# Round-by-round order in the first layer's batched stage, and reordered copies at the border of the linear layers

## The chip, the cores and the metric

The kernel runs on one core of one Trainium2 chip. The metric is the device time of one execution in microseconds (us). Seven executions of the kernel before lie between 3771.52 and 3776.72 us; their median is 3774.59 us. One execution was also taken with the hardware profiler, and every duration in this document that is not called a median comes from such a profiled execution.

## What is computed

Four layers act in turn on x of 2048 rows by 640: attention with a recurrent memory (A), linear attention (B), A again, B again. Each adds its result to x and takes the layer norm of x as input. Cut to what matters here:

```
def _A_ref(x, mem0, Wq, Wk, Wv, Wo, seg_len):      # 64 segments of 32 rows, 8 memory rows, 32 heads of 192
    mem = mem0
    for s in range(n_seg):
        h = concatenate([mem, xs])                  # 40 rows by 640
        q, k, v = h @ Wq, h @ Wk, h @ Wv            # 640 to 6144 each
        p = softmax(where(mask, q k^T * scale, -1e9))
        o = (p v) @ Wo
        mem = o[:8]; outs.append(o[8:])

def _B_ref(x, wqkv, w_phi, wo):                     # 32 heads of 20
    q, k, v = x @ wqkv
    phi_q, phi_k = softmax features of q and k, both signs
    o = (phi_q (phi_k^T v)) / (phi_q sum(phi_k))
    return o @ wo
x = x + A(layernorm(x)); x = x + B(layernorm(x))    # twice
```

The memory rows make the segments of an A layer a chain: segment s+1 needs the output of segment s.

## The kernel before

**The A layer has two stages.** A segment has 8 memory rows and 32 rows of x. The memory rows and the first 24 rows are projected in the chain; the last 8, the "tail" rows, do not depend on the memory and are projected ahead for many segments at once. `A_pre` does that: it takes the tail rows of 32 segments (256 rows, called a half, h = 0 or 1) through Wk, Wq and Wv. The weights are cut into four rounds r of 8 heads. One half with one round is called a half-round here: 12 groups of matmuls for K and Q (line 787, 10 matmuls of 128x256 a group), 8 groups for V (line 804, 5 matmuls of 128x384 a group), so 20 PSUM banks to empty. There are 8 PSUM banks in the pool. `evict` empties a bank by a copy, VectorE (line 87) and ScalarE (line 89) in turn. After K and Q of a half-round ScalarE's queue issues one write of `kqb` to memory (line 793, 1536 KB); after each V pair GpSimd's queue issues four writes of `vb` (line 808). `A_chain` then runs the 64 segments one after another; it is most of the kernel.

**The order of `A_pre` is written by hand** (`manual_schedule`). Before the change the loop over halves is outside and the loop over rounds inside: half 0 takes rounds 0, 1, 2, 3, half 1 takes 3, 2, 1, 0. `load_matrix` issues the weights of a round on SP's queue as the code reaches it. Most pieces have a home of their own; three of the five pieces of each matrix for rounds 0 and 3 share a slot, so that what round 3 put into the slots is replaced by round 0 at the very end (9 loads again).

**Layer norm as tasks.** In the first layer the norms are made inside this stage. `tails(1)` loads the tail rows of half 1 (line 691, four loads on ScalarE's queue and four on GpSimd's), `all_rows` norms all 16 blocks of 128 rows. One block is four tasks: load, moments (line 221 on VectorE, 225 and 227 on GpSimd), deviation (lines 234 and 235 on ScalarE), apply and store (lines 241 to 244, store on GpSimd, line 747). After every evict one task is taken from the list: 2 blocks of tails and 16 of rows are 72 tasks. Blocks use two buffers in turn. In the kernel before, the list is filled when half 0 comes to its third round. At the start of a half its rows are transposed by two groups of five matmuls (line 166), whose banks go out through the same copies; every group of that half needs them.

**A semaphore for a DMA.** DMAs that SP and ScalarE issue share eight semaphores, given out in one sequence for both queues; the instruction that issues a DMA waits until the last DMA with that semaphore has landed. This is in the built program's wait lists, as software sets them.

**The border to a B layer.** `post_steps` finishes the tail rows of the A layer at the head of `layer_B`. For each of four blocks tb of 16 segments, `fetch` loads `otb` (line 1117, SP) into `ot` and copies it into the layout `ow` (four copies on VectorE and ScalarE, lines 87 and 89); `multiply` runs 96 matmuls (lines 1129 and 1130), copies the result out (lines 1132 and 1133) and stores it (line 1135, SP). Blocks use two buffers in turn. Beside this, `norm_rows` (line 359 loads attention rows on SP, line 360 adds on GpSimd, then the norm; the last scaling is line 246 on ScalarE) prepares the rows of group 0, and `turn_rows` transposes them: 5 matmuls of line 166 into one of three banks, emptied on ScalarE (line 89). Here a scheduler decides the order on the engines, from data dependence and its own estimate of time, so rows of group 1 can be put before those of group 0 wherever it thinks them ready. Groups are 512 rows; the body of the layer is `for g in range(NG)`.

Of the kernel before, what the change touches and what calls it, by code (L numbers as in the profile page):

```python
# [8 lines left out]
P = 128  # L9
BF16 = mybir.dt.bfloat16  # L10
F32 = mybir.dt.float32
# [104 lines left out]
class Kernel:  # L116
# [131 lines left out]
    def layer_B(self, x_dram, at_dram, xout_dram, xnext_dram, li, bp, post):  # L248
# [44 lines left out]
        with tc.tile_pool(name=f"B{li}_kv", bufs=1, space=bass.MemoryType.PSUM, reuse_waits="tile") as kvp, \  # L293
# [71 lines left out]
            def turn_rows(b, xn, xnT):  # L365
                pt = bank("ps_x", BF16)
                for k in range(KC):
                    self.transp(out=pt[:, P * k:P * k + P], in_=xn[:, P * k:P * k + P], identity=self.ident[:, :])
                q = P * (b % 4)
                self.ev.copy(out=xnT[:, :, q:q + P], in_=pt[:, 0:D].rearrange("p (k t) -> p k t", t=P), eng="s")  # L370

            def new_xnT():
                return xnTs.next().rearrange("p (k t) -> p k t", k=KC)
# [1 line left out]
            def norm_T(g):  # L375
                xnT = new_xnT()
                load_rows(g)
                for b in range(4 * g, 4 * g + 4):
                    turn_rows(b, norm_rows(b), xnT)
                return xnT  # L380
# [73 lines left out]

            with tc.issue_after(self.last_load.ins):
                load_rows(0)
            fetch, multiply = post
            ow = [fetch(tb) for tb in range(2)]
            for j in (1, 2, 0):
                nc.sync.dma_start(out=wqkv[:, :, D * j:D * j + D],  # L460
                                  in_=self.B_wqkv.rearrange("(k p) n -> p k n", p=P)[:, :, D * j:D * j + D])
            multiply(0, ow[0], kv_ps[0], side_bank("ps_post"))
            ow.append(fetch(2))
            rows = [norm_rows(b) for b in range(4)]
            multiply(1, ow[1], kv_ps[1], side_bank("ps_post"))
            ow.append(fetch(3))
            multiply(2, ow[2], kv_ps[0], side_bank("ps_post"))
            first_xnT = new_xnT()
            for b in range(4):
                turn_rows(b, rows[b], first_xnT)  # L470
            multiply(3, ow[3], kv_ps[1], side_bank("ps_post"))
            waiting = None
            for g in range(NG):
                xnT = first_xnT if g == 0 else norm_T(g)
                if g == 1:
                    late_constants()
                keys_values(g, xnT)
                if waiting is not None:
                    query_features(*waiting)
                waiting = (g, heads_T(xnT, 0, "qT"))  # L480
# [179 lines left out]
    def A_pre(self, xn_dram, li, load_matrix, piece, wo_mid, wo_end, lay_out_wo, early_wo, x_raw):  # L660
# [3 lines left out]
        NR = 4  # L664
# [8 lines left out]
        with ExitStack() as es:  # L673
# [14 lines left out]
            def gather(dst, src, h, k):  # L688
                xv = src.rearrange("(s t) d -> t s d", t=32)
                for t2 in range(TP):  # L690
                    (nc.gpsimd if k % 2 else nc.scalar).dma_start(out=dst[SH * t2:SH * t2 + SH, :], in_=xv[24 + TP * k + t2, SH * h:SH * h + SH])

            def columns(h):
                return xT[h][:, 0:KC * T].rearrange("p (b t) -> p b t", t=T)
# [38 lines left out]
            def evict(out, in_):  # L733
                ev.copy(out=out, in_=in_)
                if tasks:
                    tasks.pop(0)()
# [3 lines left out]
            def tails(h):  # L740
                return in_turn([norm_tasks(lambda x, k=k: gather(x, x_raw, h, k),
                                           lambda xn, k=k: normed.__setitem__((h, k), xn), "ln_xt") for k in range(NT)])
# [13 lines left out]
                    for f in step:  # L756
                        f()
            turn = nv = 0
            for h in range(NH):
                xBT = columns(h)  # L760
                for k in range(NT):
                    if x_raw is not None:
                        xb = normed[h, k]
                    else:
                        xb = xB[h][k % 2]
                        gather(xb, xn_dram, h, k)
                    transpose_rows(xb, h, k)

                if h == NH - 1:
                    lay_out_wo()  # L770
                for ri, r in enumerate(range(NR) if h == 0 and NH > 1 else range(NR - 1, -1, -1)):
                    st = sts[turn % 2]
                    turn += 1
                    if x_raw is not None and h == 0 and ri == 1:
                        self.build_A_consts()
                    if x_raw is not None and h + 1 < NH and ri == 2:
                        tasks += tails(h + 1)
                        tasks += all_rows()
                    for mi, m in enumerate("KQ"):
                        load_matrix(m, r)  # L780
                        w = [piece(m, r, b) for b in range(KC)]
                        for c0 in range(0, 12, CB):
                            ps = ps_.tile([P, 512], F32, name="ps_pre", tag="bank")
                            for i in range(CB):
                                c = c0 + i
                                for b in range(KC):
                                    nc.tensor.matmul(ps[:, T * i:T * i + T], lhsT=w[b][:, P * c:P * c + P], rhs=xBT[:, b, :],
                                                     start=(b == 0), stop=(b == KC - 1))
                            G, xi = c0 // 6, c0 % 6
                            so = st[:, :, 96 * mi:96 * mi + 96].rearrange("p s (i g t) -> p i g s t", g=2, t=8)  # L790
                            evict(out=so[:, xi:xi + CB, G],
                                  in_=ps[:, :].rearrange("p (i t s) -> p i s t", i=CB, t=8))
                    nc.scalar.dma_start(out=self.kqb_d[SH * h:SH * h + SH, :, r, :].rearrange("s p f -> p s f"), in_=st)
                    load_matrix("V", r)
                    if h == NH - 1 and ri == NR - 1:
                        early_wo()
                    w = [piece("V", r, b) for b in range(KC)]
                    for k in range(NT):
                        vt = vts[nv % 2]
                        nv += 1  # L800
                        for g in range(4):
                            ps = ps_.tile([P, 512], F32, name="ps_pre", tag="bank")
                            for b in range(KC):
                                nc.tensor.matmul(ps[:, 0:384], lhsT=xBT[:, b, P * k:P * k + P],
                                                 rhs=w[b][:, 384 * g:384 * g + 384], start=(b == 0), stop=(b == KC - 1))
                            evict(out=self.two_heads(vt[:, g, :]), in_=ps[:, 0:384].rearrange("p (e f) -> p e f", e=2))
                        for t2 in range(TP):
                            nc.gpsimd.dma_start(out=self.vb_d[SH * h:SH * h + SH, r, :, TP * k + t2, :],
                                                in_=vt[SH * t2:SH * t2 + SH, :, :].rearrange("p (g x) f -> p g (x f)", x=2))
            assert not tasks  # L810
        if x_raw is None:
            self.small.close()
# [295 lines left out]
    def post_steps(self, ops):  # L1108

        nc = self.nc  # L1110
        at_dram, wo_mid, wo_end, low = self.post_args
        wo = [wo_end[:, :], wo_mid[:, 0:7680], wo_mid[:, 7680:15360], low[:, 0:7680]]

        def fetch(tb):
            o = 7680 + 12288 * (tb % 2)
            ot = low[:, o:o + 6144].rearrange("p (s f) -> p s f", f=384)
            nc.sync.dma_start(out=ot, in_=self.otb_d[16 * tb:16 * tb + 16].rearrange("s p f -> p s f"))
            ow = low[:, o + 6144:o + 12288].rearrange("p (c q) -> p c q", q=P)
            for k in range(4):
                self.ev.copy(out=ow[:, 12 * k:12 * k + 12, :].rearrange("p c (s t) -> p c s t", t=8),  # L1120
                             in_=ot[:, :, 96 * k:96 * k + 96].rearrange("p s (c t) -> p c s t", t=8))
            return ow

        def multiply(tb, ow, p0, p1):
            for c in range(48):
                lhsT = ow[:, c, :]
                w0 = 640 * (6 * (c % 2) + c % 12 // 2)
                w = wo[c // 12][:, w0:w0 + 640]
                nc.tensor.matmul(p0[:, :], lhsT=lhsT, rhs=w[:, 0:512], start=(c == 0), stop=(c == 47))  # L1129
                nc.tensor.matmul(p1[:, 0:128], lhsT=lhsT, rhs=w[:, 512:640], start=(c == 0), stop=(c == 47))  # L1130
            ob = ops.tile([P, 640], BF16, name="obB", tag="obB", bufs=2)
            nc.vector.tensor_copy(out=ob[:, 0:512], in_=p0[:, :])
            nc.scalar.activation(out=ob[:, 512:640], in_=p1[:, 0:128], func=ACT.Copy)
            av = at_dram.rearrange("(s t) d -> s t d", t=32)
            nc.sync.dma_start(out=av[16 * tb:16 * tb + 16, 24:32, :], in_=ob[:, :])

        return fetch, multiply


# [33 lines left out]
```

## Time and profile before

| what | value |
|---|---|
| median of seven runs | 3774.59 us |
| the profiled execution's own time | 3773.25 us |
| span of its profile | 3771.5 us |
| TensorE busy | 3549.9 us (94% of the span) |
| VectorE, ScalarE, GpSimd busy | 2362.1, 2074.8, 1664.9 us |
| mean granted TensorE clock | 0.977 |
| A_pre of the first layer, first to last matmul | 14.65 to 211.2 us |
| four multiplies and the transposes, first border | 1597.9 to 1661.4 us |
| four multiplies and the transposes, second border | 3459.0 to 3523.9 us |

The span runs from the first to the last instruction; 1.75 us of the execution lie around it. In a timeline, a line gives start, duration, engine, source line, operation, output and input, shape and how many were merged, and in square brackets how long the engine had stood idle and what ended that. "ACTq" and "SPq" are issues of DMAs on an engine's queue. Times of one stage can be compared line by line; a share of the whole span hides a stage that takes 5% of it.

### The profile page before, as it was taken

Reading aid. Unit: us, or ns where it says so; the run is one execution under the profiler, and the core shown is the slowest. Engines: PE = TensorE matmul, PEld = TensorE weight load, DVE = VectorE, ACT = ScalarE, POOL = GpSimd, SP = SyncE. Lnnn points to the kernel's source line nnn. Section 1 sums busy time; section 2 is a strip of 40 time slices with the busy share of each in tenths; the row PEclk is TensorE's granted clock in tenths of the full one; section 3 lists DMA queues with packets and bytes.
Section 4 is the critical chain, followed back from the end, with each engine's and each line's share of the span. In section 5 each row is a group of like instructions: output and inputs, shape, how many; then the busy total and the mean of one; then the engine's idle time right before and its main releaser. Section 6 shows DMA issues by size and latency. Waiting matters only on the chain. (4 is left out here: it accounts for less than half of the span.)

```text
span 3771.5 us, 169092 instructions
## 1 busy us (share of the span) xinstructions
PE 3549.9 (94%) x71064; PEld 2321.1 (62%) x71408; DVE 2362.1 (63%) x6290; ACT 2074.8 (55%) x5285; POOL 1664.9 (44%) x4367
## 2 busy tenths in 40 slices
PE   7889999999999999989899899999999999999798
PEld 5666666666666666645367566666666666665453
DVE  3546666666666666545643566666666666664565
ACT  2246666656666666536432566666666666664453
POOL 2435555555555555430342455555555554554300
PEclk9989999999999999989899999999999999999899
DMA  9778787878888787840376878888787887889100
GB/s 327 245 253 294 272 298 274 294 276 281 295 281 295 273 293 277 309 127 1 125 252 197 298 275 286 288 280 293 276 294 273 291 283 276 294 279 313 50 1 29
DMA packets 532613, 935.26 MB, mean 248 GB/s; under 512 B 141178, under 2 KB 298378, under 8 KB 531850
## 3 DMA queue, kind: packets, MB, share of 16 engines
q1 hardware_dynamic: 393898, 805.73, 60.2%
q0 software_dynamic: 68288, 88.95, 7.8%
q10 hardware_dynamic: 69664, 29.76, 3.0%
q8 instruction: 558, 9.14, 1.0%
q14 instruction: 205, 1.68, 0.1%
HBM read 855.97 MB, written 72.09 MB: 246 GB/s over the span
## 5 line engine op out<-in xcount | busy, mean ns | idle before, releaser
L885 PE MATMUL ps_qk<-arena,hT 128*32 128x384 bf16 x20480 | 1001.1, 328 | 22.4 <-DMA arena<-in_A_Wk_dram 7.9
L885 PEld LDWEIGHTS <-hT 128*32 128x32 bf16 x30720 | 738.0, 96 | 440.3 <-DVE hT L1103 28.9
L895 ACT ACTIVATE raw<-ps_qk 128x384 bf16<-128x384 f32 x1024 | 503.0, 491 | 391.7 <-PE ps_s L993 250.3
L961 PE MATMUL ps_w<-arena,OT 128*32 128x160 bf16 x24576 | 541.5, 235 | 23.2 <-issue 14.6
L868 POOL DMA_DIRECT2D Vp<-vb x512 | 258.7, 505 | 656.8 <-PE ps_o L935 452.3
L885 PE MATMUL ps_v<-arena,hT 128*32 128x384 bf16 x10240 | 535.5, 329 | 0.0
L961 PEld LDWEIGHTS <-OT 128*32 128x32 bf16 x24576 | 435.2, 97 | 115.9 <-issue 38.5
L900 DVE STREAM_TRANSPOSE KT<-raw 128x384 bf16<-128x384 bf16 x512 | 296.1, 578 | 202.2 <-ACT raw L895 198.2
L903 DVE STREAM_TRANSPOSE QT<-raw 128x256 bf16<-128x256 bf16 x512 | 227.9, 445 | 239.4 <-ACT raw L895 198.0
L856 POOL DMA_DIRECT2D kqb<-kqb x512 | 290.0, 566 | 165.7 <-POOL KT L864 148.1
L916 DVE CAST Vp<-ps_v 64x384 bf16<-64x384 f32 x512 | 286.2, 559 | 89.5 <-ACT Vp L914 76.3
L954 POOL DMA_DIRECT2D otb<-otb x512 | 282.5, 552 | 115.8 <-DVE otb L950 98.3
L914 ACT ACTIVATE Vp<-ps_v 64x384 bf16<-64x384 f32 x512 | 246.3, 481 | 148.0 <-PE ps_v L885 109.0
L941 DVE CAST OT<-ps_o 128x192 bf16<-128x192 f32 x512 | 183.2, 358 | 215.9 <-PE ps_o L935 198.1
L1000 DVE TENSOR_TENSOR E<-E,ps_s 80x320 bf16<-80x320 bf16 x512 | 247.5, 483 | 73.5 <-ACT ps_s L999 69.5
L979 ACT ACTIVATE E<-ps_s 80x320 bf16<-80x320 f32 x512 | 221.9, 433 | 126.7 <-PE ps_s L927 98.4
L935 PEld LDWEIGHTS <-Vp 80*128 80x128 bf16 x4096 | 183.7, 99 | 160.2 <-issue 121.6
L935 PE MATMUL ps_o<-E,Vp 80*128 80x80 bf16 x4096 | 234.3, 202 | 26.2 <-ACT Vp L914 5.7
L927 PE MATMUL ps_s<-QT,KT 128*80 128x80 bf16 (+1 forms) x3072 | 234.0, 213 | 20.3 <-DVE KT L900 11.6
L849 ACT ACTIVATE Vp<-ps_w 32x160 bf16<-32x160 f32 x512 | 150.7, 294 | 171.2 <-DVE wt L1102 151.6
L940 ACT ACTIVATE OT<-ps_o 128x192 bf16<-128x192 f32 x512 | 167.8, 328 | 140.0 <-PE ps_o L935 140.0
L927 PEld LDWEIGHTS <-KT 128*80 128x80 bf16 x3072 | 195.9, 119 | 69.1 <-issue 60.4
(148 smaller groups left out, 5468.1 us busy)
## 6 DMA issues: line engine op xcount, KB each, us to landing
arena<-wo_rows SPq DMA_DIRECT2D x792, 320.0 KB, 6.8
arena<-in_A_Wq_dram SPq DMA_DIRECT2D x430, 384.0 KB, 4.5
arena<-in_A_Wv_dram SPq DMA_DIRECT2D x430, 384.0 KB, 6.4
arena<-in_A_Wk_dram SPq DMA_DIRECT2D x768, 192.0 KB, 4.7
kqb<-arena ACTq DMA_DIRECT2D x16, 1536.0 KB, 8.7
kqb<-kqb POOLq DMA_DIRECT2D x512, 48.0 KB, 5.1
arena<-in_A_Wk_dram SPq DMA_DIRECT2D x46, 384.0 KB, 7.3
vb<-arena POOLq DMA_DIRECT2D x128, 112.0 KB, 5.5
```

The costliest lines, as they stand in the source:

```text
L856: nc.gpsimd.dma_start(out=kqb[:], in_=self.kqb_d[s, :, r, :])
L868: nc.gpsimd.dma_start(out=Vs[n % 2][64:80, :], in_=self.vb_d[s, r].rearrange("g t f -> (g t) f"))
L885: nc.tensor.matmul(o[32 * g:32 * g + 32, 0:384], lhsT=hT[:, b, :], rhs=rhs, start=(i == 0), stop=(i == KC - 1), tile_position=(0, 32 * g), ...
L895: nc.scalar.activation(out=raw[:], in_=ps[:, 0:384], func=ACT.Copy)
L900: nc.vector.transpose(out=KT[:, :, 0:64], in_=raw[:, :].rearrange("p (c j) -> p c j", j=64))
L914: nc.scalar.activation(out=o, in_=i, func=ACT.Copy)
L916: nc.vector.tensor_copy(out=o, in_=i)
L927: nc.tensor.matmul(S[0:80, c0:c0 + 80 * (q1 - q0)], lhsT=KT[:, 3 * x + i, :], rhs=QT[:, x, q0:q1, :], start=False, stop=(x == 1 and i == 2 ...
L935: nc.tensor.matmul(O[x][:, 80 * i:80 * i + 80], lhsT=Vs[n % 2][0:80, 448 * x + k:448 * x + k + 128], rhs=E[0:80, 160 * x + 80 * e:160 * x ...
L954: nc.gpsimd.dma_start(out=self.otb_d[s, :, 96 * r:96 * r + 96], in_=otb[:, :, :].rearrange("p c t -> p (c t)"))
L961: nc.tensor.matmul(W[32 * g:32 * g + 32, 0:160], lhsT=OT[:, c, q:q + 32], rhs=w[:, 640 * i + 160 * g:640 * i + 160 * g + 160], start=(firs ...
L1000: nc.vector.tensor_tensor(out=E[0:80, 0:320], in0=E[0:80, 0:320], in1=rc, op=ALU.mult)
```

## The change

1. In the first layer, `A_pre` walks `(h, r)` with the rounds outside and both halves inside: rounds 3, 2, 1, 0, each for half 0 and then half 1. The other A layer keeps its old order. The nine repeated loads are gone, since both halves use a round's weights before the slots change.
2. The list of norm tasks is filled at the very first half-round. Half 1 is transposed at the second half-round. The rewrite of Wo (two DMAs of 1920 KB from ScalarE's queue) is issued at the fifth half-round, again half-way.
3. At both borders `fetch` is split: `fetch` is the load of `otb`, `spread` the four copies. Loads 2 and 3 stand before the loads of `wqkv`; they wait until the copies of blocks 0 and 1 have read the buffers.
4. The norm of group 1 stands in `issue_after(turned.ins)`: it is scheduled after the last copy of `turn_rows` of group 0, which `turn_rows` now returns.

```diff
+                return self.ev.copy(out=xnT[:, :, q:q + P], ...)
...
-            fetch, multiply = post
-            ow = [fetch(tb) for tb in range(2)]
+            fetch, spread, multiply = post
+            ot = [fetch(tb) for tb in range(2)]
+            ow = [spread(tb, ot[tb]) for tb in range(2)]
+            ot += [fetch(tb) for tb in range(2, 4)]
             for j in (1, 2, 0):
                 nc.sync.dma_start(out=wqkv[...], in_=self.B_wqkv...)
             multiply(0, ow[0], kv_ps[0], side_bank("ps_post"))
-            ow.append(fetch(2))
+            ow.append(spread(2, ot[2]))
             rows = [norm_rows(b) for b in range(4)]
             multiply(1, ow[1], kv_ps[1], side_bank("ps_post"))
-            ow.append(fetch(3))
+            ow.append(spread(3, ot[3]))
             multiply(2, ow[2], kv_ps[0], side_bank("ps_post"))
             for b in range(4):
-                turn_rows(b, rows[b], first_xnT)
+                turned = turn_rows(b, rows[b], first_xnT)
             multiply(3, ow[3], kv_ps[1], side_bank("ps_post"))
             for g in range(NG):
-                xnT = first_xnT if g == 0 else norm_T(g)
+                if g == 0:
+                    xnT = first_xnT
+                elif g == 1:
+                    with tc.issue_after(turned.ins):
+                        xnT = norm_T(g)
+                else:
+                    xnT = norm_T(g)
...
-            for h in range(NH):
+            if x_raw is not None:
+                steps = [(h, ri, NR - 1 - ri) for ri in range(NR) for h in range(NH)]
+            else:
+                steps = [(h, ri, ri if h == 0 and NH > 1 else NR - 1 - ri) for h in range(NH) for ri in range(NR)]
+            seen = set()
+            for h, ri, r in steps:
+                if h not in seen:
+                    seen.add(h)
+                    ... gather (other layer), transpose_rows(xb, h, k) ...
+                if (h, ri) == ((NH - 1, 0) if x_raw is None else (0, 2)):
+                    lay_out_wo()
...
-                    if x_raw is not None and h + 1 < NH and ri == 2:
-                        tasks += tails(h + 1)
-                        tasks += all_rows()
+                if x_raw is not None and (h, ri) == (0, 0):
+                    for h1 in range(1, NH):
+                        tasks += tails(h1)
+                    tasks += all_rows()
```

## The prediction, as put on record

> **What bounds the kernel now.** I read the page first, then the list of TensorE's pieces in order of time for the stages that the change touches, then the other engines at TensorE's gaps.
>
> ```profile
> PE   7889999999999999989899899999999999999798
> PEclk9989999999999999989899999999999999999899
> ```
>
> TensorE is busy nearly everywhere; the chains of segments, which fill most slices, keep their code. The change can act only in the first two slices (A_pre of the first layer) and at the two borders (slices 17 and 37), all dips. In A_pre, TensorE shows:
>
> ```profile
> 55.64 11.08 PE L787 MATMUL ps_pre<-arena 128*128 128x256 bf16 x100
> 74.76 4.43 PE L787 MATMUL ps_pre<-arena 128*128 128x256 bf16 x20 [8.03 <-ACT arena L89]
> ...
> 113.31 0.44 PE L166 MATMUL pt<-ident,ln_xt 128*128 128x128 bf16 x5 [1.55 <-DVE arena L87]
> 122.90 15.53 PE L787 MATMUL ps_pre<-arena 128*128 128x256 bf16 x120 [9.15 <-ACT arena L89]
> ```
>
> Two waits of 8.03 and 9.15 us, both for ScalarE's copies out of PSUM. ScalarE's own timeline says why it was late at the first:
>
> ```profile
> 66.10 7.96 ACTq L691 DMA_DIRECT2D ln_x<-in_A_x_dram  x4
> 74.11 1.08 ACT L89 ACTIVATE arena<-ps_pre 128x512 bf16<-128x512 f32 x2 [17.77 <-DMA ln_x<-in_A_x_dram]
> ```
>
> Its four loads of half 1's tails could not be issued: each waits for the semaphore of an earlier weight load, and those had only been issued at 56.1 to 62.5 and took about 11 us. So ScalarE stood 17.77 us, and when eight banks were full TensorE stood too. At the second border (the first has the same shape, 9.05 us):
>
> ```profile
> 3497.91 1.00 PE L166 MATMUL ps_x<-ident,arena 128*128 128x128 bf16 x15
> 3508.16 0.69 PE L166 MATMUL ps_x<-ident,arena 128*128 128x128 bf16 x5 [9.26 <-ACT arena L89]
> ```
>
> The fourth transpose needs a fourth bank of three. ScalarE had put group 1's norm ahead of the copy:
>
> ```profile
> 3503.87 0.29 ACT L234 ACTIVATE ln_lv<-ln_mvr,eps 128x1 f32<-128x1 f32 x1 [6.72 <-POOL ln_mvr L227]
> ...
> 3507.42 2.48 ACT L89 ACTIVATE arena<-ps_x 128x640 bf16<-128x640 bf16 x4
> ```
>
> and GpSimd's add for that norm waited for rows from memory (its 3499.37 line has 4.42 us of waiting for `attn`).
>
> **What the Trainium skill says.** "DMA: Bandwidth & Descriptors", Anatomy of one DMA: a semaphore wait happens on the issuing sequencer before dispatch. The trace agrees: the engine that issues stands (17.77 us). The same page, Issuing engines are not separate DMA queues: all queues interleave on the same 16 engines. Agrees: in the DMA view the `kqb` write takes 9.0 us at the median, 22.4 us in the stretch 45 to 56 beside the weights. "TensorE: Matmul & The Clock Gate", What's actually happening: after about 3.4 us of idling the clock halves. Agrees: after 9.15 us the 120 matmuls take 15.53 us instead of 13.26.
>
> **Part 1, A_pre round by round.** The matmuls are the same. I cut the stage before at the first matmul of each half-round (h, r), in us: (0,0) 21.4, (0,1) 19.6, (0,2) 32.8, (0,3) 22.9, half 1's transposes and the wait behind them 11.6, (1,3) 21.9, (1,2) 23.5, (1,1) 23.2, (1,0) 19.7; sum 196.5. One undisturbed half-round is 19.6. The norm tasks run from (0,2) into (1,2). In the new order they run from the first half-round into the fourth, and the transposes follow the first.
> - The 32.8 us half-round goes. Its ScalarE loads now stand after 15 weight loads at most; the built order lets them wait for the first Q pieces, issued by 7.9 and landed by about 14.5 (6.6 us at the median), when ScalarE is free (14.6). What is late next is TensorE itself.
> - The other shapes I carry over: first half-round 21.4 (tasks beside it; 8 banks of lead cover them), transposes with their wait 11.6, then 21.9, 22.9, 23.5 with tasks, then 23.2 (tasks are over, but VectorE's clearing of `Vp`, L827, stands in its queue 4.77 us for a store, as before), then 3 x 19.6 = 58.8. Sum 183.3, so 13.2 less.
> - The 9.15 us wait stays. 20 banks after the start of tasks, as 40 before, the list is at the same phase (deviation of a block); the transposes' copies stand behind a moments task that waits for its load (issue to landing 5.9 us).
> - New: the second `kqb` issue waits, by the built order, for the semaphore of weight load 46 of 60 on SP, whose predecessors wait for the first `kqb`. Load 34 goes when that has landed, about 46 to 49 (issue 31 to 35 plus some 14); 12 loads later at about 1 us each, plus 7.6 us to landing, gives 62 to 67. The issue is due at about 62. So ScalarE stands 0 to 5 us with the V copies and a deviation task behind it; eight banks cover about 6.5 us. I take 2 us of loss, ends 0 and 6.
> - Tasks now meet the first weight loads. In the busiest stretch of before, 140 to 152, their loads and stores took 8.0 and 7.7 us instead of 5.9. Two blocks share two buffers, so a block costs half of (latency + 4.3): 5.1 us a block now ((168.0 - 76.4)/18), 6.1 at 8.0. For a handful of blocks in the densest stretch I take 1 us, ends -2 and 9.
> - Nine repeated loads (131.70 to 148.27 on SP) go: they were hidden, 0. The two rewrites of Wo (22.6 us each) leave the tasks' stretch; the next reader is the end of the stage: 0. The end's loads of Wo and Wq stay, with their waits after 222.
> Part 1: -13.2 + 2 + 1 = about -10, ends +2 and -17.
>
> **Part 2, the borders, each twice.** I follow the second one in its built order.
> - The third and fourth `otb` loads go to SP at about 3458 and, after block 1's copies (3467.6 plus 2.86), 3470.5. Behind them stand `wqkv`'s three loads (2.3 us each to issue), so to 3477, landing before 3485; they are needed at 3514: 0. Behind those stands the store of block 0's rows, ready at 3473: 4 us late.
> - Block 2's copies are due at 3485, block 3's at 3498; both come earlier: 0, as before.
> - The rows of group 0: rows 0 to 2 load from 3480, landing about 3485. Row 3's load now stands behind block 1's store: 3488, landing 3492. GpSimd's queue has one add of group 1 (1.39) between rows 2 and 3, and VectorE a moments instruction of group 1 ahead of L242 of row 2. Adding the rows' steps (add 1.4, moments 0.9, casts 0.4, deviation 0.5, L242 0.4, L246 0.8) gives row 3 at about 3500.
> - ScalarE then copies the first transposed block: 3501.1, fourth transposes to 3501.6, against 3508.65: 7 us less. The wait that is left, 3.5 us, is for the last rows' norm; ends 0 and 9.
> - The last multiply took 15.26 us at a clock of 0.84 (3508.65 to 3523.91); the earlier ones 12.95. Without the long idle, 2 us less at the second border; at the first (14.12) 1.1.
> - Group 1's norm moves behind ScalarE's copies, to about 3501 to 3508, needed after keys and values of group 0: some 40 us later: 0.
> So 9 at the second border and 8 at the first: -17, ends -7 and -22.
>
> **Sum.** 3773.25 - 10 - 17 = 3746. The profiled execution is 1.3 us under the median of 3774.59, so 3747 for a median.
>
> **The rivals.**
> 1. Only the borders gain (3757): the second `kqb` issue and the tasks among the weights cost what the tails' loads cost. For it: weights keep the DMA engines 100% busy to 44. Against: from about 75 weights are all loaded, in before the slots' reloads came back.
> 2. Only A_pre gains fully, at the borders the wait changes its name (3758): rows 2 and 3, held by the later store and by group 1's add, leave 3 us a border. It needs `attn` loads of over 8 us; with loads out of the way they took 3.4.
> 3. Slower (3788): every block of the norm at 7.4 us instead of 5.1, so 18 x 2.3 = 41 us against 27 gained. One mechanism, the loads' latency among weights: above 1.5 us more a block, a latency of about 9, it outweighs everything. Against it: 140 to 152 was as full and showed 8.0.
> 4. More (3734): the transposes' wait at half 1 shrinks, as tails are ready early, and no row is late at the borders.
> 5. Nothing moves: the built order excludes it for ScalarE; 3773 only if later waits take it all.
>
> **How the numbers follow.** Forecast 0.58 (3739 to 3753), rival 1 0.16, rival 2 0.11, rival 3 0.05, rival 4 0.08, rival 5 0.02. About 0.2% (7.5 us) is what a measurement of this kernel can tell from no change. Faster takes the forecast, rivals 1, 2 and 4: 0.93; within 0.2% is rival 5 and the mild fifth of rival 3: 0.03; slower is the rest of rival 3: 0.04. The range from 3734 to 3760 leaves out rival 3, rival 5 and the outer half of rival 4.
>
> **What would show it.** Right: no ScalarE wait for `ln_x` above 3 us; a wait of some 9 us before the second half-round; the second `kqb` issue at 62 to 67; last A_pre matmul at about 201; fourth transposes under 4 us of idle at both borders, last multiply near 13 us. Wrong: blocks above 6 us each between 20 and 110; idle before the first `ps_x` transposes or before the multiplies; a chain that changes its time per segment.

## The result, and the profile after

The changed kernel takes 3754.05 us at the median (12 runs, 3749.60 to 3762.58), the kernel before 3772.87 us over the 31 runs taken beside it. The ratio is 0.9955 with a 95% interval from 0.9946 to 0.9964, so 17.0 us less (13.6 to 20.4). The forecast was 27 us less: the sign and the range (3734 to 3760) hold, but the forecast is three fifths larger than what was measured, and 3754.05 lies just outside the 3739 to 3753 that it gave itself. The profiled execution has a span of 3752.9 us against 3771.5.

Line numbers of the kernel after are 15 higher than before inside `A_pre` (787 is 802, 793 is 808) and 19 higher in `multiply`. Here is TensorE in A_pre after the change, in order of time.

```profile
35.74 0.72 PE L166 MATMUL pt<-ident,ln_xt 128*128 128x128 bf16 x10
44.60 15.27 PE L802 MATMUL ps_pre<-arena 128*128 128x256 bf16 x120 [8.14 <-ACT arena L89]
...
66.21 3.44 PE L802 MATMUL ps_pre<-arena 128*128 128x256 bf16 x30
70.14 9.98 PE L802 MATMUL ps_pre<-arena 128*128 128x256 bf16 x90 [0.49 <-ACT arena L89]
81.49 0.97 PE L819 MATMUL ps_pre<-arena 128*128 128x384 bf16 x5 [1.36 <-DVE arena L87]
83.71 2.60 PE L819 MATMUL ps_pre<-arena 128*128 128x384 bf16 x15 [1.25 <-ACT arena L89]
88.73 5.25 PE L819 MATMUL ps_pre<-arena 128*128 128x384 bf16 x20 [2.42 <-DVE arena L87]
```

The 8.03 us wait in the middle of a half-round is gone. The 9.15 us wait behind half 1's transposes has become 8.14 us and stands at 44.6 now. The half-round from 66.21 is the longest, 27.6 us, without one big wait in it. The stage ends at 198.4 (before: 211.2). ScalarE's timeline tells one thing that holds that half-round:

```profile
63.12 0.21 ACT L235 ACTIVATE ln_sd<-ln_lv 128x1 bf16<-128x1 f32 x1
68.68 0.38 ACTq L808 DMA_DIRECT2D kqb<-arena  x1
69.60 0.87 ACT L89 ACTIVATE arena<-ps_pre 128x384 bf16<-128x384 f32 x2 [6.28 <-DMA xn<-ln_xn]
```

ScalarE stood from 63.3 to 68.7 in front of the second `kqb` issue. (The bracket names a row store; e6 below names the weight load.) SP's waits between 25 and 75 us, by what ended them (us in total, times, longest), tell why that weight load was late:

```profile
SPq L625 <- DMA kqb<-arena: 15.1, 1, 15.1
```

SP's weight load stood 15.1 us for the semaphore of the first `kqb` write, which took 16.5 us to land beside the weights.

That is not the whole of it. TensorE's longest wait in this half-round, 2.42 us at 88.73, goes back to GpSimd. `build_A_consts`, GpSimd's constants for the attention mask (lines 557 to 569), belongs to the second round of half 0. Before, that was at 39.1 to 42.1 us, ahead of every task of the list; in the new order it is this half-round, 77.7 to 80.7 us, in the middle of the tasks. The next row load goes out behind it, and the moments that wait for this load stand ahead of VectorE's copy:

```profile
81.58 0.56 POOL L754 DMA_DIRECT2D ln_x<-in_A_x_dram  x1
86.99 0.89 DVE L221 BATCH_NORM_STATS2 ln_stats<-ln_x 128x6 f32<-128x320 bf16 x2 [2.29 <-DMA ln_x<-in_A_x_dram]
```

No run moves these constants, so their share of the loss is not shown.

At the second border the waits before the third and fourth transposes, and where the work behind them begins to wait:

```profile
3486.30 0.71 PE L166 MATMUL ps_x<-ident,arena 128*128 128x128 bf16 x5 [2.34 <-ACT arena L246]
3488.24 0.69 PE L166 MATMUL ps_x<-ident,arena 128*128 128x128 bf16 x5 [0.80 <-ACT arena L89]
```

From the end of the third multiplication to the start of the fourth (one early matmul of it set aside) it is 5.3 us now at both borders; it was 10.4 and 10.6. Then, a dozen us into the body of the linear layer (first line before, at the first border; second line after):

```profile
1674.76 0.47 PE L428 MATMUL kv<-arena 128*120 128x126 bf16 x2 [1.06 <-DVE arena L422]
```
```profile
1655.73 0.46 PE L428 MATMUL kv<-arena 128*120 128x126 bf16 x2 [2.96 <-DVE arena L422]
```

A wait that was 1.06 us is 2.96 us. So I measure a border not to the end of the fourth multiplication but to a point that all kernels share and where nothing of it is left over, the start of the second run of key matmuls (the 31st matmul of line 388), counted from the border's first multiplication. Before and after, at the first border, whose first multiplication is at 1597.86 and 1581.86:

```profile
1690.95 1.24 PE L388 MATMUL ps_qk<-arena 128*120 128x512 bf16 x5
```
```profile
1672.90 1.54 PE L388 MATMUL ps_qk<-arena 128*120 128x512 bf16 x5
```

That is 93.1 and 91.0 us: of 4.9 us gained by the end of the multiplication 2.1 are left.

The whole span is 18.6 us less: A_pre 12.6 (and 0.3 earlier), the first border 4.9, the second 5.7, minus 6.7 and 1.8 in the bodies of the linear layers, and 3.1 and 0.5 in the chains, whose code is the same. Not all of that is the change's: the rest of the first linear layer, after the second run of keys, took 225.3 to 226.8 us in seven of the fourteen profiles of this study, the kernel before among them, and 229.1 to 230.0 us in the other seven, among them the kernel after and e1, whose borders are those of before. So 3.8 us of the 6.7 are not the change's. Nor are the 3.1 us of the chain: with the same code it took 1383.5 us in the kernel after and 1386.9 in e9, against 1386.6 before.

### The profile page after: what moved, and what is told of

Its sections match the earlier page's. It is cut to its first block, busy times and chain, and to the rows that moved or that the text cites. A ratio compares the mean times of both kernels' runs of the same rounds, so it can differ in the third digit from the quotient of the medians.

```text
span 3752.9 us, 169123 instructions
## 1 busy us (share of the span) xinstructions
PE 3548.1 (95%) x71064; PEld 2319.1 (62%) x71408; DVE 2363.5 (63%) x6290; ACT 2075.3 (55%) x5285; POOL 1660.3 (44%) x4367
## 4 chain that ended last, share of the span: by engine, by line
PE 62%; DMA 10%; DVE 9%; ACT 7%; issue 6%; PEld 4%; POOL 2%; SPq 0%; POOLq 0%; ACTq 0%; DVEq 0%
PE ps_qk L900 19%; PE ps_w L976 9%; PE ps_v L900 8%; PE ps_o L950 5%; PE ps_s L942 4%; DMA arena<-wo_rows 4%; PEld L802 3%; DVE hT L856 3%; PE ps_s L1008 3%; PE ps_s L937 2%; PE ps_idle L983 2%; PE ps_qk L388 2%; ACT raw L910 2%; DVE E L1015 1%; PE ps_pre L802 1%
```

## The experiments

All runs in one table. "A_pre" is first to last matmul of the first layer's stage. "Border" is first multiplication to end of the fourth; "keys" is the point described above; two numbers are the two borders. Times are in us, from one profile each; the ratio is that of timed runs to the kernel before beside them. A profile can be 10 us away from the median of its runs (those of e1, e3 and e5 are the slowest of theirs, those of e2 and e6 the fastest), so stages are compared and not spans.

| run | A_pre | border | keys | ratio (95%) |
|---|---|---|---|---|
| before | 196.6 | 63.7, 65.1 | 93.1, 94.2 | 1 |
| after | 184.0 | 58.8, 59.4 | 91.0, 90.0 | 0.9955 (0.9946 to 0.9964) |
| e1 only A_pre | 187.3 | 65.0, 65.1 | 95.3, 94.2 | 0.9967 (0.9956 to 0.9978) |
| e2 only borders | 196.7 | 57.6, 59.6 | 89.2, 90.2 | 0.9989 (0.9980 to 0.9997) |
| e3 only norm held | 201.0 | 53.4, 53.4 | 94.8, 92.8 | 1.001 (1.000 to 1.002) |
| e4 only split | 198.9 | 65.1, 64.8 | 92.7, 95.0 | 0.9999 (0.9986 to 1.0011) |
| e5 before, tails on GpSimd | 193.3 | 65.1, 63.3 | 94.2, 92.7 | 0.9975 (0.9966 to 0.9984) |
| e6 after, rows later | 185.6 | 56.7, 59.6 | 89.7, 90.0 | 0.9957 (0.9940 to 0.9974) |
| e7 after, second kqb on GpSimd | 190.2 | 59.3, 56.7 | 89.8, 89.6 | 0.9953 (0.9938 to 0.9967) |
| e8 after, block 2's copy first | 188.7 | 59.0, 60.9 | 88.2, 89.3 | 0.9943 (0.9927 to 0.9958) |
| e9 after, wqkv later | 187.5 | 53.4, 53.4 | 89.2, 90.4 | 0.9964 (0.9954 to 0.9974) |
| e10 e8 and e9 together | 189.3 | 53.4, 53.4 | 88.7, 88.1 | 0.9954 (0.9940 to 0.9969) |
| e11 after, rows third, first kqb on GpSimd | 179.4 | 56.9, 61.3 | 91.3, 91.4 | 0.9954 (0.9938 to 0.9971) |
| e12 e10 and e11 together | 182.9 | 53.4, 53.4 | 86.4, 86.6 | 0.9936 (0.9922 to 0.9950) |

Unedited A_pre of the old order appears in four profiles (mean 198.3), of the new order in five (after, e1, e8, e9, e10: mean 187.4). Unedited borders of before appear six times in keys (mean 94.0), those of after ten times (after, e2, e6, e7, e11: mean 90.2). The spread of single values is 196.6 to 201.0 and 184.0 to 189.3 for A_pre, 92.7 to 95.3 and 89.2 to 91.4 for the keys; a difference inside it shows nothing by itself. The timed runs set none of the edits to the changed kernel, e6 to e12, clearly apart from it: every interval overlaps 0.9946 to 0.9964. What these runs show is in their stages.

### Which half carries it: e1 and e2

The edit of e1 is the `A_pre` part of the diff alone, that of e2 the border part alone.

> Only the order of A_pre is changed, the borders are as before. My theory: A_pre takes about 184 us instead of 196.6, the borders stay at 63.7 and 65.1 us, and the whole is 12 to 15 us under the kernel before (about 3759). Rival: the earlier weights also change the chain of segments, so that the whole moves by 18 or more, or A_pre's gain is lost in the chain and the whole moves by less than 8.

Measured: 12.5 us less (8.3 to 16.7), A_pre 187.3, borders as before. The theory holds. On the same chip the first chain took 1390.7 us in e1 and 1389.9 in e2, so these two profiles show nothing that the new order does to the chain.

> Only the borders are changed, A_pre is as before. My theory: each border (first multiplication to end of the fourth) takes about 59 us instead of 64 to 65, but 1 to 3 us of that is given back in the B layer that follows, where VectorE's moments of later groups stand ahead of the normalised values: 6 to 9 us less for the whole. Rival: the gain of the borders stays whole and is 10 to 11 us; or the bodies lose all of it and nothing is left.

Measured: 4.2 us less (1.1 to 7.6), under the 6 to 9 that I expected, though the interval reaches into it; the keys are 4.8 and 3.8 us under the mean of the old borders. The two halves together, 16.7, are what the whole change shows (17.0).

### Which part of the border change: e3 and e4

e3:

```diff
-                xnT = first_xnT if g == 0 else norm_T(g)
+                ... norm_T(1) in issue_after(turned.ins), fetch and copies as before
```

> Of the change only the norm of group 1 is held behind the last transposed copy; the copies of otb and their loads stay as before. My theory: this alone takes the 9 us wait before the fourth transpose to 3 us or less, since the row loads start at 16 us after the first multiplication and not at 27; the border is 57 to 59 us. Rival: the copies matter, and without them the third multiplication or the wait grows, 61 us or more.

Measured: the border falls further than in the changed kernel, to 53.4 us at both places, and the fourth multiplication runs in 12.98 us. And yet nothing is gained by the keys point, at the first border at least, and the timed runs are not faster at all. I did not expect that. TensorE of this run, first border:

```profile
1650.14 0.44 PE L166 MATMUL ps_x<-ident,arena 128*128 128x128 bf16 x5 [0.23 <-ACT arena L89]
1663.24 3.40 PE L388 MATMUL ps_qk<-arena 128*120 128x512 bf16 x15
1673.08 6.28 PE L388 MATMUL ps_qk<-arena 128*120 128x512 bf16 x15 [6.44 <-ACT arena L89]
...
1687.66 0.47 PE L428 MATMUL kv<-arena 128*120 128x126 bf16 x2 [2.77 <-DVE arena L422]
```

and ScalarE at the same time:

```profile
1669.83 0.29 ACT L234 ACTIVATE ln_lv<-ln_mvr,eps 128x1 f32<-128x1 f32 x1 [6.52 <-POOL ln_mvr L227]
...
1672.44 1.56 ACT L89 ACTIVATE arena<-ps_qk 120x512 bf16<-120x512 f32 x3
```

The wait of 9 us has moved into the keys. The fourth transposes wait for nothing, but the keys stop 6.44 us for ScalarE's copies, and these stand behind a norm that waits 6.52 us for GpSimd. It is the same kind of stall (a norm of a later group ahead of a copy in ScalarE's queue), one group further on: group 2 now.

e4 is the split of loads and copies alone, here against the kernel after:

```diff
-                xnT = first_xnT ... issue_after(turned.ins) ...
+                xnT = first_xnT if g == 0 else norm_T(g)
```

> Of the change only the split of load and copies is made; the norm of group 1 is not held. My theory: nothing is gained, since the copies were ready before; the 9 us wait stays, and because the weights now delay block 0's store, the border is the same or up to 3 us longer (64 to 67 us each). Rival: the split carries the gain, the border falls to about 60.

Measured: nothing, as expected. Row loads start at 28.0 and 27.4 us after the first multiplication, not at 16.4. Neither half of the border change alone is worth anything that these runs can tell; both together (e2) are worth 4 us. The difference between e3 and the kernel after that I see in the queues: block 1's result is stored 28.7 us after the first multiplication with the split, and 33.7 us without it, because its copy then stands behind the norm of group 0. Group 1's rows are read behind that store. No run tests this alone.

### The causes in A_pre: e5, e6, e7, e11

e5, in the kernel before:

```diff
-                    (nc.gpsimd if k % 2 else nc.scalar).dma_start(...)
+                    (nc.gpsimd if k % 2 or (x_raw is not None and h) else nc.scalar).dma_start(...)
```

> The kernel before, with one thing changed: half 1's four tail loads go to GpSimd's queue and not to ScalarE's, so that no weight load's semaphore is waited for. My theory (A_pre's gain is that ScalarE no longer stands for those loads): the third half-round falls from about 33 us to 21 to 24 and A_pre from 197 to about 186, 10 us of gain with the old order. Rival: the gain comes from the order itself (weights early, tasks early), and A_pre stays above 193.

Measured: the half-round of 32.8 us takes 23.0, as the theory says, and the runs are 9.4 us less (6.0 to 12.8). But A_pre is 193.3, the rival's number, 5.0 under the mean of the old order: the half-rounds behind it grew, the next one with its transposes from 34.5 to 37.9. The two do not agree: the profile is of the slowest of 21 runs, and by the timed runs this edit gains most of what e1 gains (12.5, 8.3 to 16.7). So the ScalarE stall was real and its removal pays; how much the order itself adds to that, these runs do not settle.

e6, in the kernel after:

```diff
                         tasks += tails(h1)
-                    tasks += all_rows()
+                if x_raw is not None and (h, ri) == (NH - 1, 0):
+                    tasks += all_rows()
```

> The changed kernel, with the tasks of the 16 row blocks put into the list only after half 1's transposes. My theory (the 8 us wait at these transposes is a copy standing behind moments of a row block that wait for a load): that wait falls below 2 us, the matmuls behind it run at full clock, and A_pre is 6 to 9 us shorter, unless the tasks' end, some 15 us later, now meets VectorE's clearing of buffers. Rival: the tails themselves come late, the wait stays above 5 us.

Measured: the mechanism is as stated and the gain is none. TensorE and ScalarE of this run:

```profile
36.30 0.72 PE L166 MATMUL pt<-ident,ln_xt 128*128 128x128 bf16 x10
37.81 13.26 PE L803 MATMUL ps_pre<-arena 128*128 128x256 bf16 x120 [0.79 <-ACT arena L89]
...
69.66 11.84 PE L803 MATMUL ps_pre<-arena 128*128 128x256 bf16 x90 [6.04 <-ACT arena L89]
```
```profile
68.53 0.39 ACTq L809 DMA_DIRECT2D kqb<-arena  x1
69.12 0.87 ACT L89 ACTIVATE arena<-ps_pre 128x384 bf16<-128x384 f32 x2 [9.76 <-DMA arena<-in_A_Wk_dram]
```

The wait behind the transposes falls from 8.14 to 0.79 us and the matmuls run at full clock (13.26). TensorE then reaches the third half-round 8 us earlier and stops there for 6.04 us, because the second `kqb` issue comes at 68.5 all the same: ScalarE now stands 9.76 us, and the wait's name is a weight load. That issue is at 68.5 to 70.0 in all six profiles with the new order and this write on ScalarE. As long as both first writes stay on ScalarE's queue it is a fixed point in time, and the gain ahead of it only made the wait in front of it longer.

e7, in the kernel after, moves that second write to GpSimd's queue:

```diff
-                nc.scalar.dma_start(out=self.kqb_d[...
+                (nc.gpsimd if x_raw is not None and (h, ri) == (1, 0) else nc.scalar).dma_start(out=self.kqb_d[...
```

> The changed kernel, with the second write of kqb issued on GpSimd's queue. My theory (ScalarE stands 5.3 us in the issue for the semaphore of a weight load): no such wait on ScalarE, and the third half-round falls from 27.6 to about 23 us, so A_pre 3 to 5 us shorter. Rival: the row blocks' loads (3 to 5 us waits on VectorE in that half-round) are the cause, and it stays above 26 us.

Measured: the theory fails as I put it. ScalarE is free, but the third half-round takes 30.6 us. GpSimd's waits from 60 to 85 us, in the same columns:

```profile
POOL ln_x L754 <- DMA kqb<-arena: 6.7, 1, 6.7
```

A row block's load, the eighth DMA after the write on GpSimd's queue, waits for the write to land: eight semaphores go round on that queue too. ScalarE then stands 10.79 us for a block's moments, whose casts stand behind that load on GpSimd. The wait has only changed its engine, and the rival's number (above 26 us) is what came.

e11 takes away the cause ahead of both: the first `kqb` write goes to GpSimd's queue, and the row blocks come only at the third half-round, so that nothing on GpSimd is late for it.

```diff
+                if x_raw is not None and (h, ri) == (0, 1):
+                    tasks += all_rows()
...
-                nc.scalar.dma_start(out=self.kqb_d[...
+                (nc.gpsimd if x_raw is not None and (h, ri) == (0, 0) else nc.scalar).dma_start(out=self.kqb_d[...
```

> The changed kernel, with the row blocks' tasks put into the list at the third half-round and the first kqb write issued on GpSimd's queue. My theory (the first kqb write holds SP's loads, these hold the second kqb write, which came at 68.5 to 69.7 us in every version, and that holds ScalarE): SP's weight loads no longer stop at 32 us, the second kqb issue comes at about 57 to 59 us without a wait, the waits of 8 and 6 us go, and A_pre takes 168 to 176 us. Rival: the row blocks meet other waits when they run later (VectorE's clearing, the two rewrites of Wo), and A_pre stays above 181.

Measured: 179.4, between the two. TensorE:

```profile
38.20 13.26 PE L803 MATMUL ps_pre<-arena 128*128 128x256 bf16 x120 [0.79 <-ACT arena L89]
51.29 6.66 PE L820 MATMUL ps_pre<-arena 128*128 128x384 bf16 x40
57.79 13.26 PE L803 MATMUL ps_pre<-arena 128*128 128x256 bf16 x120
71.28 7.27 PE L820 MATMUL ps_pre<-arena 128*128 128x384 bf16 x40 [0.23 <-DVE arena L87]
```

Both waits are gone, and the second `kqb` issue comes at 52.1 with no wait. Half-rounds two and three take 19.6 and 22.4. SP's weight loads no longer stop at 32 us. e6 had late rows too and its second issue stayed at 68.5, so it is the move of the first write that brings it forward. The stage is 8 us under the mean of the new order, and not 11 to 19, since the tasks now load the fourth to sixth half-round (23.1, 26.0 and 25.6 us); e12, with the same edits here, took 182.9, which is the rival's side. In time nothing of it shows: 0.9954, as the changed kernel. A load of SP still stands 14.1 us for a `kqb` write in this run, but for the second one, from 59 to 73 us, and TensorE waits only 0.23 us in that stretch.

### The borders' rest: e8, e9, e10

e8 adds VectorE's copy of block 2's result to what group 1's norm is held behind:

```diff
-                    with tc.issue_after(turned.ins):
+                    with tc.issue_after(turned.ins), tc.issue_after(ob2.ins):
```

> The changed kernel, with group 1's moments on VectorE held behind the copy of block 2's result. My theory (part of the borders' gain is given back because that copy, and so the store and group 2's rows, stand behind group 1's moments): group 2's row loads start at 43 to 45 us after the first multiplication and not at 49, the last group's adds end at about 69 and not 73, and the second run of key matmuls starts 2 to 4 us earlier than 90 to 91. The wait before the fourth transpose stays (5 us). Rival: the adds on GpSimd, not the store, set the pace, and the second run starts where it did.

Measured: group 2's rows load at 45.9 and 46.6 and not at 49.3, the last adds end at 71.2 and 73.1, keys at 88.2 and 89.3: 2.0 and 0.9 under the mean of after, a part of what I expected and in its direction. At the second border neither the adds (72.9 in the kernel after) nor the keys leave the spread of unedited profiles.

e9 puts the three loads of `wqkv` behind the first three row loads:

```diff
-            for j in (1, 2, 0):
-                nc.sync.dma_start(out=wqkv[...], ...)
...
+            with tc.issue_after(self.row_load.ins):
+                for j in (1, 2, 0):
+                    nc.sync.dma_start(out=wqkv[...], ...)
+            rows.append(norm_rows(3))
```

> The changed kernel, with the loads of wqkv issued behind group 0's first three row loads and not ahead of block 0's store. My theory (the 5.3 us left before the fourth transpose came from rows that start at 27 us, because block 0's store waits behind these loads on SP and then shares the DMA engines with them): the rows load at 18 to 21 us, the wait falls under 2 us and the fourth multiplication runs in 13 us, so each border takes 53 to 56 us; but the second run of key matmuls moves by less than 3 us, since the later groups set it. Rival: GpSimd's adds of group 1 between rows 2 and 3 make the wait, and it stays at 3 us or more.

Measured: rows load at 18.6 and 18.5, no wait before the fourth transposes, and borders of 53.4 us. So the late rows were the cause of what was left there; with the rows early, group 1's adds no longer come in front of them. As expected too, keys stay at 89.2 and 90.4: 5 to 6 us less in the border are given back before the keys. Second border:

```profile
3502.03 3.40 PE L388 MATMUL ps_qk<-arena 128*120 128x512 bf16 x15
3508.46 4.91 PE L388 MATMUL ps_qk<-arena 128*120 128x512 bf16 x15 [3.03 <-ACT arena L89]
...
3523.06 0.47 PE L428 MATMUL kv<-arena 128*120 128x126 bf16 x2 [3.57 <-DVE arena L422]
```

> As the run with wqkv's loads behind the rows, and also group 1's moments on VectorE behind the copy of block 2's result. My theory: both waits go, the borders take 53 to 56 us and the second run of key matmuls starts at 85 to 88 us after the first multiplication instead of 90 to 91. Rival: the last group's adds, behind the store of block 3 and 8 us of constants on GpSimd, stay at 71 us or later and the second run does not move by more than 2 us.

Measured: borders of 53.4, keys at 88.7 and 88.1, just outside what I expected; the last adds end at 71.5 and 69.9, so the first border fits the rival as well. The wait for the keys is gone, the one before `kv` has grown to 5.13 at the second border.

### Together: e12

> The changed kernel with both sets of edits: row blocks from the third half-round with the first kqb write on GpSimd's queue, and at the borders wqkv's loads behind the rows and group 1's moments behind block 2's copy. My theory (the stages add up, and nothing later takes them back): A_pre about 180 us instead of 184 to 189, the second key run at 88 instead of 90 to 91 after the first multiplication at both borders, so 10 to 14 us under the changed kernel, a ratio to the kernel before of 0.992 to 0.993. Rival: the granted clock takes back what the waits gave, and the ratio is 0.995 or above, as for the runs with one of the two sets.

Measured: ratio 0.9936 (0.9922 to 0.9950), 24.3 us less than before, and keys at 86.4 and 86.6. Neither number of the expectation is excluded by the interval, which overlaps that of the changed kernel (0.9946 to 0.9964) a little. The best kernel of this study is this one; that it beats the changed kernel is likely, not certain.

## Why the prediction was right or wrong, point by point

- **Right: the stall that goes.** ScalarE's wait for half 1's tails is gone, and A_pre is 12.6 us shorter in the profiles compared, 10.9 between means. I had -10. By half-round, forecast and measured: first 21.4 and 21.4; transposes with their wait 11.6 and 8.9; second 21.9 and 21.6; third 22.9 (with up to 3 us of new costs) and 27.6; fourth 23.5 and 21.6; fifth 23.2 and 24.0; the last three 58.8 and 58.9.
- **Right in kind, too small: the second `kqb` issue.** "I take 2 us of loss": it came at 68.7, not at 62 to 67, and the half-round lost 4.7. The first write took 16.5 us to land, not "some 14" (15.5 already in the kernel before). Nor need all of the 4.7 be this issue's: the prediction carried the shape over from a half-round without GpSimd's mask constants and put nothing for them. In the sum the loss was offset by a smaller wait at the transposes (2.7 us) and a shorter fourth half-round (1.9), which no term had, so that A_pre's total came out so close is in part luck. What I did not see is that the two waits are coupled: e6 shows that taking away the first only lengthens the second.
- **Right: tasks among weights.** Blocks stayed near 5 us ((115.2 - 20.7)/18 = 5.25, counted as in the prediction from the first moments to the last store). Row loads took 2.5 to 6.5 us. Rival 3 falls.
- **Wrong: "So 9 at the second border and 8 at the first".** Measured to the end of the multiplications it is 5.7 and 4.9; measured to the keys, 3.7 per border between means. Three terms of that sum failed.
  - "Rows 0 to 2 load from 3480, landing about 3485", which is 21 us after the first multiplication. They loaded at 26.9. I had the store late by 4 us for SP's queue, and left out that it then waits in the DMA engines beside 2.4 MB of `wqkv`: SP stood 5.6 us for it to land. e9 shows it: without these loads, 18.5 us and no wait. With the rows late, GpSimd's adds of group 1 came between their steps, two and not the one that I had counted (the second and fourth line):

```profile
3481.61 0.18 POOL L225 CAST ln_mv<-ln_mv 128x2 bf16<-128x2 f32 x1 [1.21 <-DVE ln_mv L223]
3481.75 1.40 POOL L360 TENSOR_TENSOR arena<-arena 128x640 bf16<-128x640 bf16 x1
3483.09 0.19 POOL L227 CAST ln_mvr<-ln_mv 128x2 f32<-128x2 bf16 x1
...
3483.34 1.40 POOL L360 TENSOR_TENSOR arena<-arena 128x640 bf16<-128x640 bf16 x1
3484.68 0.29 POOL L227 CAST ln_mvr<-ln_mv 128x2 f32<-128x2 bf16 x1
```

  - "Without the long idle, 2 us less". The fourth multiplication took 14.40 and 14.99 us, against 14.29 and 15.43 (counted to the end of the last matmul; the prediction's 14.12 and 15.26 stop where the next work starts). An interruption of 5.3 us costs the clock as one of 10 does; one of 1.35 us (e3, e9, e10, e12) does not, 12.98 or 12.99.
  - "Group 1's norm moves behind ScalarE's copies ... needed some 40 us later: 0". Group 1 was indeed not late. But group 1's moments stand ahead of block 2's copy on VectorE, that copy ahead of block 2's store, and the store ahead of group 2's rows. I followed the moved step to its own reader and not to what is queued behind it.
- **Rivals 1 and 2 had the better total.** They forecast 3757 and 3758, 17.6 and 16.6 us less; 17.0 were measured. e1 excludes rival 1, since A_pre alone gains 12.5. Rival 2 had the right place with the wrong reason. It said that the wait would change its name at the borders, with 3 us left per border. 3.7 were left. Its condition, row loads of over 8 us, did not occur: they took 2.2 us at the median, and it was the store ahead of them that was slow.
- **The sum.** -10 and -17 became -10.9 and -7.5, together -18.4; timed, -17.0.

What bounds the keys point can be read from the traces. In all 28 borders of the 14 profiles GpSimd goes without idling from its late constants (lines 317 to 328, 8.4 us) to the adds of the last group, so these adds never waited for their rows or for the last store. The first `kv` matmul starts 1.0 us after the last of these adds, each time, and the keys point comes 15.5 to 18.2 us after it. At the second border of the kernel after:

```profile
3507.78 4.02 POOL L328 TENSOR_SCALAR_AFFINE_SELECT arena<-arena 128x720 bf16<-128x720 bf16 x4
3511.78 5.43 POOL L360 TENSOR_TENSOR arena<-arena 128x640 bf16<-128x640 bf16 x4
3517.41 0.47 POOL L414 CAST arena<-rk 128x64 bf16<-128x64 f32 x1
3518.21 0.47 PE L428 MATMUL kv<-arena 128*120 128x126 bf16 x2 [2.38 <-DVE arena L422]
```

So the point follows the start of these constants: 62.1 and 63.5 us after the first multiplication before, 62.9 and 62.1 in e3, 59.1 and 59.1 in the kernel after, 55.4 and 55.6 in e12. That is why e3's border of 53.4 us gained nothing. No run takes the constants away from there, so what that would be worth is open.

What else stays open: why the tasks cost more when they run later (e11's 26.0 and 25.6), which I put to VectorE's queue from the names of the waits but did not test.

## What to carry to other kernels

A stall at an in-order queue is worth what the next common point in the program moves by, not its own length: e3 took the whole 10 us out of a border and not one us out of the kernel. When a step is moved behind another, list what stands behind it on each of its queues, and follow these to their readers. When a loop is reordered, look for small steps tied to one of its indices, as the mask constants here: they move along. In this program a DMA issue waits for whatever DMA had its semaphore last (15.1 us on SP, 9.76 on ScalarE, 6.7 on GpSimd): look for issues that come at the same absolute time in every version, since gains ahead of such a point are lost in front of it.

## What the runs showed of the hardware that was not expected

The clock after an interruption is not a matter of its length alone. Between the third and fourth multiplication, 4.60, 4.63 and 4.82 us left the fourth at full clock (12.98 to 12.99 us), while after 4.53 and 4.92 us it took 14.04 and 15.33; from 5.2 us on all took 14.29 or more. Transposes run inside these stretches; TensorE stood idle for 3.1 to 3.3 us of the first three and for 2.8 and 3.0 us of the other two, so the idle time does not order them either. The Trainium skill, "TensorE: Matmul & The Clock Gate", What's actually happening, says that the window over which activity is judged is free-running; the two outcomes near one length agree with that. The first `kqb` write, 1536 KB, took 15.1 to 17.5 us from ScalarE's queue among weight loads; the last one, of the same size, took 7.8 us at the end of the stage.
